# First batch of a windowed attention: probabilities held in the array, v with a column of ones moving, normalisation behind the product

## The chip, the cores and the metric

The kernel runs on one core of one Trainium2 chip. The metric is device time in microseconds (us) of one execution; three executions of the kernel before took 1189.88 to 1190.43 us, median 1190.07. The engines are named as in the profile: PE is TensorE's matrix array, PEld its loading of the operand that stays in the array, DVE is VectorE, ACT is ScalarE, POOL is GpSimd, SP is the queue that issues most transfers.

## The reference, cut to what matters

Attention over 4 batches, 8 heads, 768 positions, head size 64, where each query sees its last `n_local` = 96 keys and the first `n_global` = 8 keys, with a bias that falls with distance; its output feeds a mixture of 4 experts with weights given per row.

```python
scores = scale * q @ k.T + bias[head]            # -1e9 where a key is not kept
a = np.exp(scores - max(scores))
a = a / (sum(a) + 1e-9)
x = concat_heads(a @ v)                          # 3072 x 512
out = sum_e p[:, e] * (relu(x @ w1[e]) @ w2[e])
```

## The kernel before, in words

Queries are worked in tiles of 128. A tile of queries needs one window of 256 keys at most: 96 earlier keys and 32 global ones, which stand as one block of 128, and its own 128. The first tile of a head needs its own 128 alone. Two heads (a pair) are worked together, so a batch is 4 pairs of 6 tiles.

The first batch is done by itself ahead of everything else (`attention(0, A, early=True)`, called at line 916). Its result x is needed before the mixture can begin. The attention of the batches 1 to 3 runs beside the mixture's products of the batch before it, in another form that the change leaves alone. While the first batch runs, the steps (one tile each, 24 of them in the pair order 0, 2, 1, 3, and 4 more to empty the pipeline) also carry chores, at fixed step numbers (lines 917 to 928): the first expert weights are loaded and split into two parts on ACT and POOL, and the blocks of x that the mixture's products need are formed on DVE, ACT and POOL. `Ordered` keeps each engine's instructions in the order in which the program writes them, so an instruction that waits holds all that stand behind it on that engine.

The stages of one tile in the first batch, one step apart:

- `scores_early` (line 401), every second step: for two tiles and two heads, q times k on PE. k and q of 64 rows each, one head in each half of the array's rows.
- `softmax` (line 414) with the tile as `new`: one DVE instruction per head adds the bias and takes the maximum, then ACT takes the exponential and its sum (`accum_out`, which the trace shows as a second, short ACT instruction).
- `softmax` one step later with the tile as `old`: DVE adds 1e-9 to the sums, takes the reciprocal and multiplies the 256 probabilities of each head by it.
- `turn` (line 455) one step later: PE transposes the four 128x128 blocks of probabilities, ACT copies them from PSUM to pT.
- `weigh` (line 467), once in three tiles: v (128 keys x 64) stands in the array and pT (128 keys x 128 queries) moves, so the output is already x with head dimension down the partitions; the two heads use the two halves of the array's columns. One ACT copy takes 384 columns of x out of PSUM.

`prepare_early` (line 361) transposes q and k in threes on PE and copies them out of PSUM on ACT. `windows` (line 378) forms the keys' block of 96 earlier and 32 global rows of v by one transfer and one POOL copy. `load` (line 308) issues v's transfer on SP. The table `AHEAD` (line 212) says in which steps a later pair is prepared. PSUM holds one buffer for px, three for the transposes and four for the scores (line 915). fp32 products of PE appear as two instructions per product in the trace, transposes as one.

Of the kernel before, what the change touches and what calls it, by code (L numbers as in the profile page):

```python
# [9 lines left out]
F32 = mybir.dt.float32  # L10
# [3 lines left out]
AF = mybir.ActivationFunctionType  # L14
ALU = mybir.AluOpType
# [3 lines left out]
P = 128  # L19
NEG = 1.0e9  # L20

NGLOB = 32
NPREV = 96
# [163 lines left out]
def attn_moe_kernel(ctx: ExitStack, tc, q, k, v, n_global, n_local, domain_probs, w1, w2, out):  # L187
    nc = tc.nc
    B, H, S, D = q.shape
    N, E = domain_probs.shape  # L190
    DM, FF = w1.shape[1], w1.shape[2]
    NQT = S // P
# [4 lines left out]
    HALF = S // 2  # L197
# [110 lines left out]
    def load(A, src, b, pr, name, parts=1):  # L308

        if src is v:  # L310
            nat = A.natv.tile([P, 2, NQT, D], F32, name=name)
            rows = src[b, 2 * pr : 2 * pr + 2].rearrange("j (t p) d -> p (j t) d", p=P)
            sy.dma_start(nat.rearrange("p j t d -> p (j t) d"), rows)
            yield nat
            return
        nat = A.nat.tile([P, NQT, 2, D], F32, name=name)
        for hf in range(parts):
            ts = slice(hf * NQT // parts, (hf + 1) * NQT // parts)
            for j in range(2):
# [38 lines left out]
        if hf == 0:  # L358
            ve.tensor_copy(kd[:, :, :, P:], f32(kd[:, :, 0:1, :NGLOB]).to_broadcast([P, 2, NQT, NGLOB]))

    def prepare_early(A, nat, hf, name, got):

        tp = transpose_half(A, nat, hf)
        tpv = tp[:, :HALF].rearrange("p (t c) -> p t c", c=P)
        pl = slice(hf * TPH, (hf + 1) * TPH)
        if name == "q":
            if hf == 0:
                got["q"] = A.qd.tile([P, NQT, P], F32, name="early_q")
            ac.activation(got["q"][:, pl, :], tpv, AF.Copy, scale=-SCALE)
            return  # L370
        if hf == 0:
            got["k"] = A.kd.tile([P, NQT, PL], F32, name="early_k")
        dst = got["k"]
        ac.copy(dst[:, pl, :P], tpv)
        if hf == 0:
            po.tensor_copy(dst[:, :, P:], dst[:, 0:1, :NGLOB].to_broadcast([P, NQT, NGLOB]))

    def windows(A, vt):

        vg = A.vg.tile([P, 2, NQT, D], F32, name="vg")  # L380
        sy.dma_start(vg[:NPREV], vt[NGLOB:])
        po.tensor_copy(vg[NPREV:], vt[:NGLOB, :, 0:1, :].to_broadcast([NGLOB, 2, NQT, D]))
        return vg

    def scores(A, t, got):
# [15 lines left out]
    def scores_early(A, t0, got):  # L401
# [9 lines left out]
                te.matmul(heads[j][:, t - t0, :n], got["q"][own, t, :], win, start=True, stop=True)  # L411
        return [[heads[j][:, i] for j in range(2)] for i in range(2)]

    def softmax(A, new, old):


        if old:
            pb, zsum = old["pb"], old["zsum"]
        if new:
            t, pr, ps = new["t"], new["pr"], new["ps"]  # L420
            cols = slice(0, P) if t == 0 else slice(0, 2 * P)
            bcol = slice(2 * P, 3 * P) if t == 0 else slice(0, 2 * P)
            new["pcol"] = pcol = slice(P, 2 * P) if t == 0 else slice(0, 2 * P)
            nmax = A.small.tile([P, 2], F32, name="nmax")
            new["zsum"] = A.small.tile([P, 2], F32, name="zsum")
            new["pb"] = A.pb.tile([P, 2, 2 * P], F32, name="pb")
        for j in range(2):
            if new:
                e = new["pb"][:, j, pcol]
                ve.tensor_tensor_reduce(  # L430
                    e, ps[j][:, cols], nbias[:, 2 * pr + j, bcol], 1.0, 3.0e38, ALU.add, ALU.min, nmax[:, j : j + 1]
                )
                ac.activation(
                    e, e, AF.Exp, bias=nmax[:, j : j + 1], scale=-1.0, accum_out=new["zsum"][:, j : j + 1]
                )
            if old:
                if j == 1:
                    ve.reciprocal(zsum, zsum)
                elif A.early:

                    old["spare"] = spare = A.small.tile([P, 3], F32, name="spare")
                    ve.tensor_scalar(zsum, zsum, 1e-9, None, op0=ALU.add, op1=ALU.add, accum_out=spare[:, 2:3])
                else:
                    ac.activation(zsum, zsum, AF.Copy, bias=1e-9)
        if old:
            for j in range(2):
                p = pb[:, j, old["pcol"]]
                if A.early:
                    ve.tensor_scalar(
                        p, p, zsum[:, j : j + 1], None, op0=ALU.mult, op1=ALU.add, accum_out=old["spare"][:, j : j + 1]  # L450
                    )
                else:
                    ac.activation(p, p, AF.Copy, scale=zsum[:, j : j + 1])
# [12 lines left out]

    def weigh(A, three, x):

# [18 lines left out]
    def attention(b, A, early=False):  # L487


        x = xs[b] = xp.tile([P, NPAIR, S], F32, name="x")  # L490
        tiles, turned, ahead = [None] * 4, [], [None]

        def flow(new=None):

            one, two, three, four = tiles
            if new:
                if not early:
                    new["ps"] = scores(A, new["t"], gots[new["pr"]])
                elif new["t"] % 2 == 0:
                    new["ps"], ahead[0] = scores_early(A, new["t"], gots[new["pr"]])  # L500
                else:
                    new["ps"] = ahead[0]
            if four:
                turned.append(four)
            ready = len(turned) == TPH
            if ready and not early:
                weigh(A, turned, x)
            if three and not early:
                turn(A, three)
            softmax(A, one, two)  # L510
            if three and early:
                turn(A, three)
            if ready and early:
                weigh(A, turned, x)
            if ready:
                turned.clear()
            tiles[:] = [new, one, two, three]

        def start(pr):
# [17 lines left out]

        def prepare_all(pr):

            nat, got = nats[pr], gots[pr]  # L540
            got["v"] = nat
            prepare_early(A, nat["q"], 0, "q", got)
            if pr:
                yield 1
            prepare_early(A, nat["k"], 0, "k", got)
            yield 1
            nat["vg"] = windows(A, nat["v"])
            prepare_early(A, nat["k"], 1, "k", got)
            yield 1
            prepare_early(A, nat["q"], 1, "q", got)  # L550
            yield 1

        nats, gots = {}, [{} for _ in range(NPAIR)]
# [463 lines left out]
```

## Time and profile before

| | |
|---|---|
| median of three runs | 1190.07 us (1189.88 to 1190.43) |
| span of the profiled execution | 1189.2 us |
| instructions | 18,091 |
| PE busy | 1164.3 us, 98% of the span |
| PEld busy | 1039.9 us, 87% |
| DVE busy | 825.8 us, 69% |
| ACT busy | 494.4 us, 42% |
| POOL busy | 210.7 us, 18% |
| HBM | 190 GB/s over the span |

The page gives no time for the profiled execution but its span from first to last instruction; the median of the runs is 0.87 us above that span. The span has two parts. To about 63 us the first batch's attention runs by itself with the chores; after it the mixture's products fill PE to the end. A busy PE in the profile need not be PE at its peak, since each instruction's time holds the array's latency and neighbours overlap; how closely instructions follow one another is read from their start times in the timeline.

### The profile page before, as it was taken

How to read it: one execution, taken by the hardware profiler on the slowest of the kernel's cores; microseconds unless marked ns; L12 is line 12 of the kernel's file. 1: busy time of each engine (PE TensorE's matmuls, PEld its weight loads, DVE VectorE, ACT ScalarE, POOL GpSimd, SP SyncE). 2: the span in 40 equal slices, each digit the busy share in tenths (PEclk: the TensorE clock that was granted, in tenths of full speed). 3: DMA queues.
4: the chain of work that ended last, by engine and by line, in shares of the span. 5: the costliest groups of instructions: out<-in, count | busy, mean ns of one | idle time of the engine just before them, and what ended most of it. 6: DMA issues, size and time to landing. Idle time of an engine off the chain costs nothing.

```text
span 1189.2 us, 18091 instructions
## 1 busy us (share of the span) xinstructions
PE 1164.3 (98%) x6624; PEld 1039.9 (87%) x6624; DVE 825.8 (69%) x1859; ACT 494.4 (42%) x1268; POOL 210.7 (18%) x221
## 2 busy tenths in 40 slices
PE   7789999999999999999999999999999999999998
PEld 5579899898989898998988998989988999999996
DVE  7887676776687666666758867666666766666665
ACT  7955655565533444444432444444444211111110
POOL 4755665555230000000001000000001000000000
PEclk9999999999999999999999999999999999999999
DMA  8486897878578566666657657575654645554532
GB/s 200 160 246 243 306 299 264 258 278 298 178 244 275 186 209 198 201 217 213 183 178 242 237 198 219 164 238 192 206 186 154 234 188 195 195 187 177 186 133 91
DMA packets 122703, 251.38 MB, mean 211 GB/s; under 512 B 83184, under 2 KB 91376, under 8 KB 106224
## 3 DMA queue, kind: packets, MB, share of 16 engines
q1 hardware_dynamic: 118864, 243.87, 61.8%
q10 hardware_dynamic: 3744, 6.30, 1.4%
q8 instruction: 54, 0.88, 0.3%
q14 instruction: 41, 0.34, 0.1%
HBM read 174.11 MB, written 52.43 MB: 190 GB/s over the span
## 4 chain that ended last, share of the span: by engine, by line
PE 90%; DMA 3%; ACT 3%; DVE 2%; POOL 1%; issue 1%; SPq 0%; POOLq 0%; DVEq 0%
PE pm L43 80%; PE pt L43 6%; PE ps L43 3%; DMA qd<-st_q 2%; ACT pb L43 1%; DVE pb L43 1%; DMA raw<-in_moe_w_dram 1%; POOL w1s L43 0%; DMA q<-in_q_dram 0%; ACT xT L43 0%; ACT pT L43 0%; SPq L43 0%; DVE x L43 0%; ACT w1s L43 0%; POOL w2s L43 0%
## 5 line engine op out<-in xcount | busy, mean ns | idle before, releaser
L43 PE MATMUL pm<-w2s,h 128*128 128x512 f32 x2304 | 551.6, 393 | 1.5 <-DVE h L43 1.5
L43 PEld LDWEIGHTS pm<-w2s,h 128*128 128x128 f32 x2304 | 426.1, 188 | 89.4 <-DVE h L43 3.1
L43 DVE SCALAR_TENSOR_TENSOR acc<-pm,prob,acc 128x512 f32<-128x512 f32 x360 | 267.8, 749 | 151.6 <-PE pm L43 149.7
L43 PE MATMUL pm<-xT,w1s 128*128 128x384 f32 x1536 | 296.0, 337 | 1.7 <-DVE vv L43 1.0
L43 PEld LDWEIGHTS pm<-xT,w1s 128*128 128x128 f32 x1536 | 266.3, 188 | 5.2 <-issue 1.7
L43 PE MATMUL pm<-xB,w1s 128*128 128x384 f32 x1146 | 225.2, 338 | 0.2 <-DVE xB L43 0.2
L43 PEld LDWEIGHTS pm<-xB,w1s 128*128 128x128 f32 x1146 | 200.4, 188 | 5.1 <-issue 0.5
L43 ACT ACTIVATE h<-pm 128x384 fp32r<-128x384 f32 x256 | 124.7, 491 | 176.5 <-DVE pm L43 172.8
L43 DVE SCALAR_TENSOR_TENSOR h<-pm,h 128x384 fp32r<-128x384 f32 x256 | 140.5, 551 | 10.9 <-ACT h L43 7.7
L43 ACT ACTIVATE pb<-pb,nmax 128x256 f32<-128x256 f32 (+1 forms) x192 | 93.8, 495 | 92.1 <-DVE nmax L43 91.2
L43 ACT COPY p<-pm 128x384 f32<-128x384 f32 x63 | 30.2, 479 | 185.8 <-PE pm L43 176.9
L43 POOL COPY vg<-v 32x768 f32<-32x768 f32 x16 | 13.5, 843 | 505.5 <-DMA v<-in_v_dram 440.4
L43 DVE TENSOR_TENSOR u<-pm,p 128x384 f32<-128x384 f32 x64 | 35.6, 557 | 71.2 <-PE pm L43 58.1
L43 DVE CUSTOM_DVE_ANT_0 pb<-ps,nbias 128x256 f32<-128x256 f32 (+1 forms) x192 | 71.5, 396 | 8.3 <-PE ps L43 4.8
L43 ACT COPY pT<-pt 128x512 f32<-128x512 f32 (+1 forms) x96 | 53.4, 556 | 53.6 <-PE pt L43 53.4
L43 DVE TENSOR_TENSOR pm<-pm,vv 128x384 f32<-128x384 f32 x128 | 71.6, 560 | 1.5 <-PE pm L43 1.3
L43 ACT ACTIVATE pb<-pb,zsum 128x256 f32<-128x256 f32 (+1 forms) x144 | 63.3, 484 | 17.9 <-DVE zsum L43 17.8
L43 PE MATMUL pt<-ident,pb 128*128 128x128 f32 x352 | 57.4, 278 | 7.7 <-DVE pb L43 5.4
L43 PEld LDWEIGHTS pt<-ident,pb 128*128 128x128 f32 x352 | 42.1, 141 | 17.8 <-ACT pb L43 3.3
L43 DVE TENSOR_TENSOR vv<-pm,u 128x384 f32<-128x384 f32 x64 | 35.6, 557 | 27.3 <-PE pm L43 26.9
L43 DVE TENSOR_TENSOR u<-pm,u 128x384 f32<-128x384 f32 x64 | 35.6, 557 | 27.1 <-PE pm L43 26.5
L43 POOL TENSOR_TENSOR w2s<-raw,w2s 128x512 fp32r<-128x512 f32 x32 | 40.9, 1293 | 44.8 <-ACT w2s L43 44.7
(91 smaller groups left out, 881.3 us busy)
## 6 DMA issues: line engine op xcount, KB each, us to landing
w1s<-kept SPq DMA_DIRECT2D x48, 1792.0 KB, 7.3
w2s<-kept SPq DMA_DIRECT2D x48, 1024.0 KB, 4.8
kept<-w1s SPq DMA_DIRECT2D x16, 1792.0 KB, 7.9
qd<-st_q SPq DMA_DIRECT2D x96, 192.0 KB, 5.0
raw<-in_moe_w_dram SPq DMA_DIRECT2D x32, 512.0 KB, 4.7
kept<-w2s SPq DMA_DIRECT2D x16, 1024.0 KB, 6.6
v<-in_v_dram SPq DMA_DIRECT2D x16, 384.0 KB, 4.0
out_dram<-acc ACTq DMA_DIRECT2D x24, 256.0 KB, 3.4
```

Source lines behind the costliest of these rows:

```text
L43: ins = fn(*args, **kwargs)
```

## The change

In the first batch alone, the probabilities are no longer normalised before they are transposed. The transposed probabilities (128 keys x 128 queries) now stand in the array and v moves, 64 columns and one more that holds ones; so the output has queries down the partitions, 64 columns of unnormalised x and one of the sum, for each of the two heads. Once in three tiles DVE adds 1e-9 to the sums, takes the reciprocal and multiplies the three tiles' x by it; PE then transposes x back in three transposes in the step after, and DVE (for the last pair ACT) copies it to x. The exponential no longer sums. q and k of all pairs but the first are copied out of PSUM by DVE where ACT did it. v's tile has 65 columns per head and tile, and POOL writes the ones. The other batches' code is the same as before (in `softmax` only the branch for the first batch is taken out).

```diff
     def load(A, src, b, pr, name, parts=1):
         if src is v:
-            nat = A.natv.tile([P, 2, NQT, D], F32, name=name)
+            nat = A.natv.tile([P, 2, NQT, D + 1 if A.early else D], F32, name=name)
             rows = src[b, 2 * pr : 2 * pr + 2].rearrange("j (t p) d -> p (j t) d", p=P)
-            sy.dma_start(nat.rearrange("p j t d -> p (j t) d"), rows)
+            if A.early:
+                po.memset(nat[:, :, :, D:], 1.0)
+            sy.dma_start(nat[:, :, :, :D].rearrange("p j t d -> p (j t) d"), rows)
...
-    def prepare_early(A, nat, hf, name, got):
+    def prepare_early(A, nat, hf, name, got, lead):
...
-            ac.activation(got["q"][:, pl, :], tpv, AF.Copy, scale=-SCALE)
+            if lead:
+                ac.activation(got["q"][:, pl, :], tpv, AF.Copy, scale=-SCALE)
+            else:
+                ve.tensor_scalar_mul(got["q"][:, pl, :], tpv, -SCALE)
...
-        ac.copy(dst[:, pl, :P], tpv)
+        if lead:
+            ac.copy(dst[:, pl, :P], tpv)
+        else:
+            ve.tensor_copy(dst[:, pl, :P], tpv)
...
+    def exponentials(A, new, j):
...
+        ve.tensor_tensor_reduce(e, ps[j][:, cols], nbias[:, 2 * pr + j, bcol], 1.0, 3.0e38, ALU.add, ALU.min, nmax)
+        if A.early:
+            ac.activation(e, e, AF.Exp, bias=nmax, scale=-1.0)
+        else:
+            ac.activation(e, e, AF.Exp, bias=nmax, scale=-1.0, accum_out=new["zsum"][:, j : j + 1])
...
-                    ve.tensor_scalar(zsum, zsum, 1e-9, None, op0=ALU.add, op1=ALU.add, accum_out=spare[:, 2:3])
...
-                    ve.tensor_scalar(
-                        p, p, zsum[:, j : j + 1], None, op0=ALU.mult, op1=ALU.add, accum_out=old["spare"][:, j : j + 1]
-                    )
...
+    def weigh_early(A, tile_, px):
+
+        t, pT = tile_["t"], tile_["pT"]
+        vt, vg = tile_["v"]["v"], tile_["v"]["vg"]
+        for j in range(2):
+            for w in range(1 if t == 0 else 0, 2):
+                vv = vt[:, j, t] if w == 1 else vg[:, j, t - 1]
+                te.matmul(
+                    px[:, t % TPH, j], pT[:, w, j, :], vv, start=(w == 1 if t == 0 else w == 0), stop=(w == 1)
+                )
+
+    def normalise(A, px):
+
+        z = A.small.tile([P, TPH, 2, 1], F32, name="z")
+        xn = A.pb.tile([P, TPH, 2, D], F32, name="xn")
+        ve.tensor_scalar_add(z, px[:, :, :, D:], 1e-9)
+        ve.reciprocal(z, z)
+        ve.tensor_tensor(xn, px[:, :, :, :D], z.to_broadcast([P, TPH, 2, D]), op=ALU.mult)
+        return xn
+
+    def turn_values(A, xn, x, pr, hf):
+
+        tp = A.pt.tile([P, 512], F32, name="pt")
+        for i in range(TPH):
+            te.transpose(tp[:, i * P : (i + 1) * P], xn[:, i].rearrange("p j d -> p (j d)"), ident)
+        dst = x[:, pr, hf * HALF : (hf + 1) * HALF]
+        if pr == PAIRS[-1]:
+            ac.copy(dst, tp[:, :HALF])
+        else:
+            ve.tensor_copy(dst, tp[:, :HALF])
...
+        def flow_early(new=None):
+
+            one, two, three, four = tiles
+            if normed:
+                turn_values(A, *normed.pop())
+            if new:
+                if new["t"] % 2 == 0:
+                    new["ps"], ahead[0] = scores_early(A, new["t"], gots[new["pr"]])
+                else:
+                    new["ps"] = ahead[0]
+            if one:
+                for j in range(2):
+                    exponentials(A, one, j)
+            if two:
+                turn(A, two)
+            if three:
+                if three["t"] % TPH == 0:
+                    ahead.append(A.px.tile([P, TPH, 2, D + 1], F32, name=A.pxname))
+                weigh_early(A, three, ahead[1])
+                if three["t"] % TPH == TPH - 1:
+                    normed.append((normalise(A, ahead.pop()), x, three["pr"], three["t"] // TPH))
+            tiles[:] = [new, one, two, three]
```

`windows` takes v's new width (65) for its tile, its transfer and its POOL copy, and `prepare_all` passes `lead`, true for the first pair.

## Rows read from the trace of the kernel before

**Rows 1.** The profile's page: the span and the busy time of each engine.
```profile
span 1189.2 us, 18091 instructions
PE 1164.3 (98%) x6624; PEld 1039.9 (87%) x6624; DVE 825.8 (69%) x1859; ACT 494.4 (42%) x1268; POOL 210.7 (18%) x221
```

**Rows 2.** The chain of work that ended last, its last piece (start, length, what).
```profile
918.78 264.67 PE pm L43 x1320
```

**Rows 3.** Busy time of each engine in stretches of 10 us; after the stretch and its length stand PE, PEld, DVE, ACT and POOL, each with its instructions, then the granted clock, DMA's share and GB/s.
```profile
20.00:30.00 10.00, 9.87 (x95) 7.58 (x95) 9.31 (x61) 10.00 (x36) 4.04 (x5) 1.00 0.75 191
...
40.00:50.00 10.00, 6.73 (x48) 4.48 (x46) 8.30 (x39) 8.23 (x27) 8.78 (x10) 0.83 0.84 322
```

**Rows 4.** PE's timeline in the first batch, from the first transposes of probabilities to the end of the stage (start us, length us, engine, line, operation, out<-in, shapes, count); a next group's start less this group's start is what the group took of PE.
```profile
12.59 0.50 PE L43 MATMUL pt<-ident,pb 128*128 128x128 f32 x2 [0.27 <-DVE pb L43]
...
21.02 1.13 PE L43 MATMUL ps<-early_k,early_q 64*128 64x256 f32 x8
...
23.22 0.44 PE L43 MATMUL px<-pT,vg 128*64 128x128 f32 x4
...
24.68 0.55 PE L43 MATMUL pt<-ident,k 128*128 128x128 f32 x3
25.16 1.13 PE L43 MATMUL ps<-early_k,early_q 64*128 64x256 f32 x8
26.23 0.66 PE L43 MATMUL pt<-ident,pb 128*128 128x128 f32 x4
26.72 0.49 PE L43 MATMUL pt<-ident,q 128*128 128x128 f32 x3
27.05 0.60 PE L43 MATMUL pt<-ident,pb 128*128 128x128 f32 x4
...
31.89 1.14 PE L43 MATMUL ps<-early_k,early_q 64*128 64x256 f32 x8
...
59.91 1.30 PE L43 MATMUL ps<-xB,w1s 128*128 128x384 f32 x6
61.06 0.85 PE L43 MATMUL pt<-ident,pb 128*128 128x128 f32 x4
...
63.34 0.97 PE L43 MATMUL pm<-xB,w1s 128*128 128x384 f32 x4
```

**Rows 5.** ACT's timeline in one step of the first batch (columns as in the group before).
```profile
25.81 0.53 ACT L43 COPY early_k<-pt 128x384 f32<-128x384 f32 x1
26.18 0.57 ACT L43 ACTIVATE pb<-pb,nmax 128x256 f32<-128x256 f32 x1
26.59 0.25 ACT L43 ACTIVATION_READ_ACCUMULATOR pb<-pb,nmax 128x1 f32 x1
26.68 0.56 ACT L43 ACTIVATE pb<-pb,nmax 128x256 f32<-128x256 f32 x1
...
27.18 0.63 ACT L43 COPY pT<-pt 128x512 f32<-128x512 f32 x1
27.64 0.56 ACT L43 ACTIVATE early_q<-pt 128x384 f32<-128x384 f32 x1
```

**Rows 6.** DVE's groups of instructions between 9 and 64 us, different shapes apart (busy us, mean ns of one, idle before).
```profile
L43 DVE TENSOR_SCALAR_CACHE_REDUCE pb<-pb,zsum 128x256 f32<-128x256 f32 x40 | 17.6, 477 | 0.7
...
L43 DVE RECIPROCAL zsum<-zsum 128x2 f32<-128x2 f32 x24 | 3.8, 159 | 0.0
L43 DVE TENSOR_SCALAR_CACHE_REDUCE zsum<-zsum 128x2 f32<-128x2 f32 x24 | 3.6, 151 | 4.6 <-ACT pb L43 4.4
```

**Rows 7.** The costliest groups of instructions on the page (busy us, mean ns of one, idle before): loads and products of the mixture, and a DVE instruction that reads 384 columns of PSUM.
```profile
L43 PE MATMUL pm<-w2s,h 128*128 128x512 f32 x2304 | 551.6, 393 | 1.5 <-DVE h L43 1.5
L43 PEld LDWEIGHTS pm<-w2s,h 128*128 128x128 f32 x2304 | 426.1, 188 | 89.4 <-DVE h L43 3.1
...
L43 DVE TENSOR_TENSOR u<-pm,p 128x384 f32<-128x384 f32 x64 | 35.6, 557 | 71.2 <-PE pm L43 58.1
```

**Rows 8.** Instructions that write the tiles px and ps in the first 64 us: count, shortest/median/longest duration in ns, first and last start, shapes.
```profile
L43 PEld LDWEIGHTS px<-pT,v x96: 132/137/232, 18.5 to 63.0; 128*64 128x64 f32 x96
L43 PE MATMUL px<-pT,v x96: 272/273/473, 18.5 to 63.1; 128*64 128x128 f32 x96
...
L43 PEld LDWEIGHTS ps<-early_k,early_q x96: 182/187/335, 7.4 to 53.3; 64*128 64x128 f32 x96
L43 PE MATMUL ps<-early_k,early_q x96: 272/376/792, 7.4 to 53.5; 64*128 64x256 f32 x80, 64*128 64x128 f32 x16
```

**Rows 9.** PE's timeline in the mixture: four products of scores of the later batches, 256 columns moving, between products of 512 columns.
```profile
89.63 0.64 PE L43 MATMUL ps<-kd,qd 128*128 128x256 f32 x4
90.10 1.09 PE L43 MATMUL pm<-w2s,h 128*128 128x512 f32 x4
```

**Rows 10.** ACT's timeline at and behind the end of the stage.
```profile
63.46 0.48 ACT L43 COPY x<-px 128x384 f32<-128x384 f32 x1 [0.34 <-PE px L43]
...
71.16 0.62 ACT L43 CAST w2s<-raw 128x512 fp32r<-128x512 f32 x1 [0.82 <-DMA raw<-in_moe_w_dram]
```

**Rows 11.** The timeline of loads (PEld) where a group of px begins behind transposes.
```profile
29.41 0.20 PEld L43 LDWEIGHTS px<-pT,v 128*64 128x64 f32 x4 [0.17 <-issue]
```

**Rows 12.** POOL's timeline: the first of its chores on the expert weights and the last in this stage.
```profile
31.92 0.73 POOL L43 TENSOR_TENSOR sums<-raw 128x256 f32<-128x256 f32 x1 [6.30 <-DMA raw<-in_moe_w_dram]
...
61.44 1.27 POOL L43 TENSOR_TENSOR w1s<-sums,w1s 128x512 fp32r<-128x512 f32 x1
```

More of the change, by code (lines that the diff above doesn't have):

```diff
@@ L412, in scores_early @@
         return [[heads[j][:, i] for j in range(2)] for i in range(2)]
-    def softmax(A, new, old):
[L417 to L426, printed above, removed]
+    def exponentials(A, new, j):
+        t, pr, ps = new["t"], new["pr"], new["ps"]
+        cols = slice(0, P) if t == 0 else slice(0, 2 * P)
+        bcol = slice(2 * P, 3 * P) if t == 0 else slice(0, 2 * P)
+        if j == 0:
+            new["pcol"] = slice(P, 2 * P) if t == 0 else slice(0, 2 * P)
+            new["nmax"] = A.small.tile([P, 2], F32, name="nmax")
+            new["pb"] = A.pb.tile([P, 2, 2 * P], F32, name="pb")
+            if not A.early:
+                new["zsum"] = A.small.tile([P, 2], F32, name="zsum")
+        e, nmax = new["pb"][:, j, new["pcol"]], new["nmax"][:, j : j + 1]
+        ve.tensor_tensor_reduce(e, ps[j][:, cols], nbias[:, 2 * pr + j, bcol], 1.0, 3.0e38, ALU.add, ALU.min, nmax)
[3 more added lines that the diff above has]
+            ac.activation(e, e, AF.Exp, bias=nmax, scale=-1.0, accum_out=new["zsum"][:, j : j + 1])
@@ L427, in softmax @@
+    def softmax(A, new, old):
         for j in range(2):
             if new:
[L429 to L435 removed]
+                exponentials(A, new, j)
@@ L490, in attention @@
         x = xs[b] = xp.tile([P, NPAIR, S], F32, name="x")
-        tiles, turned, ahead = [None] * 4, [], [None]
-        def flow(new=None):
+        tiles, turned, ahead, normed = [None] * 4, [], [None], []
+        def flow_early(new=None):
             one, two, three, four = tiles
+            if normed:
+                turn_values(A, *normed.pop())
             if new:
-                if not early:
-                    new["ps"] = scores(A, new["t"], gots[new["pr"]])
-                elif new["t"] % 2 == 0:
+                if new["t"] % 2 == 0:
                     new["ps"], ahead[0] = scores_early(A, new["t"], gots[new["pr"]])
@@ L502, in flow @@
                     new["ps"] = ahead[0]
+            if one:
[10 more added lines that the diff above has]
+            tiles[:] = [new, one, two, three]
+        def flow(new=None):
+            if early:
+                return flow_early(new)
+            one, two, three, four = tiles
+            if new:
+                new["ps"] = scores(A, new["t"], gots[new["pr"]])
             if four:
                 turned.append(four)
-            ready = len(turned) == TPH
-            if ready and not early:
+            if len(turned) == TPH:
                 weigh(A, turned, x)
-            if three and not early:
+                turned.clear()
+            if three:
                 turn(A, three)
             softmax(A, one, two)
[L511 to L516, printed above, removed]
             tiles[:] = [new, one, two, three]
```

28 lines of the change are left out of this document (12 added, 16 removed).

## The prediction, made before the changed kernel was run

> **What bounds the kernel now.** I read the page first: PE is busy 98% of the span [rows 1], so the change can matter only where PE has gaps or gets other work. The chain of waits ends in 264.67 us of nothing but products [rows 2]; the mixture behind the first batch is PE from end to end, and the change leaves its products alone. So the time moves by what the first batch's stage, which ends at about 63 us, gets shorter or longer.
>
> In that stage the table of stretches names two engines. From 20 to 30 us ACT is busy 10.00 of 10 and PE 9.87; from 40 to 50 PE is down to 6.73 and the granted clock to 0.83 [rows 3]. As "busy" counts overlapped latency, I went on to the starts in PE's timeline [rows 4]. Eight instructions of scores take 25.16 to 26.23 = 1.07 us, four transposes 26.23 to 26.72 = 0.49, three of q or k 26.72 to 27.05 = 0.33, and 24 of px 23.22 to 24.68 = 1.46, or 0.061 each. The six tiles from 21.02 to 31.89 need 3 x 1.07 + 22 x 0.122 + 44 x 0.061 + 6 x 0.33 = 10.6 us of such work, in 10.87 us. So in the first half PE is as full as ACT. Over the stage, from the first transposes of probabilities at 12.59 to the last px, behind which the next product starts at 63.34, PE has 50.75 us and needs: scores 10 x 1.07 = 10.7, transposes 88 x 0.122 = 10.8, px 176 x 0.061 = 10.7, twelve groups of q and k 4.0, the opening product 59.91 to 61.06 = 1.15; together 37.4 us. The other 13.4 us are waits and a slow clock, nearly all in the second half, where ACT and POOL carry the chores.
>
> **What the change takes away.** On ACT the short instruction behind each exponential goes: from exponential to exponential it is 0.50 us with it, 26.18 to 26.68, and 0.41 up to its start at 26.59 [rows 5]; 0.09 x 48 = 4.3 us. Twelve copies of q and k (25.81 to 26.18 = 0.37) and six of x go to DVE: 18 x 0.37 = 6.7 us. An attention tile then costs ACT 2 x 0.41 + 0.46 = 1.3 us. On DVE two multiplications of 477 ns, the 1e-9 (151) and the reciprocal (159) go per tile [rows 6], some 1.26 us. In come, per three tiles, 1e-9, reciprocal and one multiplication (557 by an instruction that reads 384 columns of PSUM [rows 7]), and the 18 copies, 0.56 each by the same row: (0.87 x 8 + 0.56 x 18) / 24 = 0.71 per tile. Both engines are relieved. Where PE is the bound that is worth nothing; in all it is worth at most PE's 13.4 us.
>
> **What it adds on PE: the pace of px.** The count of 176 instructions stays. Before, 64 columns of v are loaded and 128 columns move, and the two heads share the array. After, 128 columns are loaded and 65 move, and each product takes the whole array. Moving: 128 columns take 273 ns and 256 take 376 [rows 8], 0.8 ns a column, so 65 columns stream in about 53 ns, which is per product what two at a time cost today. Loading: 64 columns take 137 ns and 128 take 187 [rows 8], again 0.8 ns a column, so 128 columns stream in about 100 ns. No row shows a load longer than the product that covers it. Bounds: 0.061, today's pace, if the load doesn't count, and 0.153, if load and product follow one another. The nearest row has a 128-column load behind a stream of about equal length: four products in 89.63 to 90.10, 0.118 each [rows 9]. That loads hide behind products is seen where 188 ns of load vanish under products of 512 columns [rows 7]. I take 0.118: 176 x (0.118 - 0.061) = +10.0 us.
>
> The Trainium skill speaks against this change: "TensorEngine Tiling (Array Packing)", section Performance Considerations, says that where the moving side has 64 columns or fewer the operands are to be swapped and the array's columns split, which is how the kernel stands before. "TensorE: Matmul & The Clock Gate", section LDWEIGHTS (loading the stationary operand), gives columns / 1.2 ns; an estimate by that page is 107 ns for 128 columns, and the term would be 176 x (0.107 - 0.061) = +8.1 in place of +10.0. The 50 ns between the loads of 64 and 128 columns agree with it.
>
> **The transposes back.** Eight groups of three, 0.33 each [rows 4]: +2.6 us.
>
> **A new wait.** PE keeps program order, and the transposes back stand at the head of the step behind normalisation. They wait for the last px's latency (273 ns less 53 for 63 columns fewer: 0.22), for DVE's 0.15 + 0.16 + 0.56 [rows 6, 7] and for two hand-overs of 0.05, as from px to the copy of x at 63.46 [rows 10], an estimate: 1.19, less 0.1 for px's own slot, 1.1 us. Behind them on PE stand that step's scores, transposes and px, and ACT and DVE wait for those. Eight times is 8.8; in three of the eight the table AHEAD puts three transposes of q or k (0.33) in between: +7.8 us. Bounds: 0, if other work of PE fills it all, and 9 to 10, if DVE is late with its copies. In the kernel before normalisation lies a step ahead of the transposes and costs PE little while it is full.
>
> **What comes back.** With no split columns the 0.17 us of idle loading ahead of a px group [rows 11] should go: 8 x 0.17 = -1.4 us; bounds 0 and twice that, were the way back as dear.
>
> **Small edits.** POOL's writes of ones hold v's loads on SP. The fourth pair's must wait until the first pair's v is free; behind it stand k's global columns on POOL and the expert weights' first loads on SP, which arrive some 2 us later for it. POOL's chores, 31.92 to 62.71 [rows 12], would begin later and are covered by PE's later end. If PE were not late, that cover were gone: POOL is busy 8.78 us of 10 from 40 on [rows 3], so its chain can shrink little, and a stage that ended before about 60 would meet it. The wider copy and transfer of v's window (780 columns for 768) I take as nothing; POOL hides it.
>
> **Sum.** 37.4 + 10.0 + 2.6 + 7.8 - 1.4 = 56.4 us, from 12.6: the last transposes end at 69.0 and the copy of x starts 0.2 later, at 69.2, where it starts at 63.46 now [rows 10]: +5.75. This leaves PE no other wait, as both other engines need under 2 us a tile for 2.35 on PE. Behind the stage, ACT waits 0.82 us for a weight load [rows 10] whose issue hangs on an earlier step and not on the end; I take 0.5 back. The span gets 5.25 longer, 1194.45; the median lies 0.87 above the span now, so the time is **1195.3 us**. All terms are at full clock; the slow stretch after 40 us [rows 3] came with PE's gaps, which go.
>
> **Rivals.**
> 1. *Faster: the load does not pace px.* If 128 columns of load hide as 64 do today, px stays at 0.061, and the end moves by 5.25 - 10.0 = -4.75: 1185.3, or up to 1188 where POOL's chores then hold it. For it: loads of 137 ns already follow at 0.061. Against it: the 0.118 [rows 9]. The sign turns at 0.118 - 5.25 / 176 = 0.088. Chance 0.20.
> 2. *Much slower: load and product take turns.* At 0.153, 176 x 0.035 = 6.2 more: 1201.5. The Trainium skill's "TensorE: Matmul & The Clock Gate", Part 3, lets a load overlap a running product in other rows of the array or in a background buffer; its first half alone would make it this rival. For it: every load is now to the whole array. Against it: the 188 ns hidden under products of the whole array [rows 7]. Chance 0.10.
> 3. *Nothing to be measured: the new work falls into the 13.4 us.* The second half's waits for ACT and POOL stay, and its half of the added work (10 us) lies beside them; the first half's lies beside the wait for normalisation where AHEAD fills it. End at +1 to +2: 1191.5. Against it: in my sum the relief of ACT takes those waits away first. Chance 0.10.
>
> The forecast has 0.60, from 1192 (pace 0.107, the new wait 0.9) to 1199 (pace 0.13, DVE late with its copies).
>
> **How the numbers follow.** The forecast's own 1192 to 1199 leaves out 4 in 10. To hold 8 the range takes in rival 3, half of rival 1 down to 1186.5, and rival 2 up to 1202. A measurement of this kernel tells 0.2%, 2.4 us, from no change. Slower: the forecast but 0.05 at its low end, and rival 2: 0.65. Within: that 0.05, rival 3 and nothing of rival 1 but its POOL-bound end, 0.03: 0.18. Faster: the rest of rival 1: 0.17.
>
> **What would show it.** Right: px instructions about 0.12 us apart with loads of 187 ns; eight idle times of PE of about a microsecond ahead of the transposes of xn, put down to DVE; ACT with idle time between 20 and 30 us; the scores that start at 31.89 [rows 4] some 7 us later; the last copy of x at about 69. Wrong: px 0.06 apart; PE waiting for ACT, POOL or DVE's chores in the second half as now; or a last copy of x at 63 or before.

## The result: slower by 12 us, more than twice what was forecast

The changed kernel takes 1202.28 us (median of 4 runs, 1200.85 to 1204.60) where the kernel before takes 1190.25 on the same chip: ratio 1.0097, 95% interval 1.0082 to 1.0112. The forecast was 1195.3, range 1186.5 to 1202.0: the sign holds, the size does not, and the time lies 0.3 us above the range. The profiled run took 1200.85 us with a span of 1198.1.

The page after, against [rows 1], and the last piece of its chain, against [rows 2]: the span has grown by 8.9 us, and the last run of products starts 8.93 later and is as long as before. So all of it lies ahead.

```profile
span 1198.1 us, 17947 instructions
```

```profile
927.71 264.65 PE pm L43 x1320
```

Stretches of the stage, columns as in [rows 3]. Between 20 and 30 us ACT has fallen from 10.00 to 4.01 and DVE from 9.31 to 6.47: the relief is there. But PE has fallen as well, from 9.87 to 8.86, and the low clock, in the kernel before at 42 to 48 us, is still there, at 51 to 57. The first line below is the kernel before, the others the changed one.

```profile
42.00:45.00 3.00, 3.00 (x22) 2.47 (x24) 2.96 (x13) 3.00 (x12) 1.99 (x2) 0.52 0.83 350
```

```profile
20.00:30.00 10.00, 8.86 (x76) 7.58 (x76) 6.47 (x25) 4.01 (x10) 4.79 (x6) 1.00 0.68 151
...
51.00:54.00 3.00, 2.98 (x16) 2.16 (x17) 2.19 (x7) 1.32 (x3) 2.51 (x3) 0.59 1.06 415
54.00:57.00 3.00, 3.00 (x25) 2.91 (x26) 2.23 (x10) 2.27 (x6) 2.74 (x4) 0.84 1.01 414
```

PE's timeline, against [rows 4]:

```profile
12.99 1.34 PE L43 MATMUL pt<-ident,pb 128*128 128x128 f32 x6
...
20.40 0.52 PE L43 MATMUL pt<-ident,xn 128*128 128x128 f32 x3 [0.83 <-DVE xn L43]
20.85 0.93 PE L43 MATMUL ps<-early_k,early_q 64*128 64x128 f32 x8
21.71 0.66 PE L43 MATMUL pt<-ident,pb 128*128 128x128 f32 x4
22.20 0.34 PE L43 MATMUL px<-vg,pT 128*128 128x65 f32 x2
22.37 0.39 PE L43 MATMUL px<-v,pT 128*128 128x65 f32 x2
...
23.04 0.50 PE L43 MATMUL pt<-ident,q 128*128 128x128 f32 x3
...
40.16 1.14 PE L43 MATMUL ps<-early_k,early_q 64*128 64x256 f32 x8
...
47.39 0.39 PE L43 MATMUL px<-v,pT 128*128 128x65 f32 x2
47.98 0.95 PE L43 MATMUL pt<-ident,pb 128*128 128x128 f32 x4 [0.20 <-ACT pb L43]
48.84 0.44 PE L43 MATMUL px<-vg,pT 128*128 128x65 f32 x2
...
49.56 0.39 PE L43 MATMUL px<-v,pT 128*128 128x65 f32 x2
51.02 0.55 PE L43 MATMUL pt<-ident,xn 128*128 128x128 f32 x3 [1.07 <-DVE xn L43]
51.50 1.65 PE L43 MATMUL ps<-early_k,early_q 64*128 64x128 f32 x8
53.08 1.11 PE L43 MATMUL pt<-ident,pb 128*128 128x128 f32 x4
53.99 0.53 PE L43 MATMUL px<-vg,pT 128*128 128x65 f32 x2
...
55.29 0.61 PE L43 MATMUL pt<-ident,pb 128*128 128x128 f32 x4
...
72.66 0.39 PE L43 MATMUL px<-v,pT 128*128 128x65 f32 x2
74.21 0.52 PE L43 MATMUL pt<-ident,xn 128*128 128x128 f32 x3 [1.16 <-DVE xn L43]
74.48 1.83 PE L43 MATMUL pm<-xB,w1s 128*128 128x384 f32 x9
```

Four things are to be seen. Eight instructions of px take 22.20 to 23.04 = 0.84 us, 0.105 each (0.111 behind the first pair: 22.37 to 23.04 for six). The last pair of px ahead of a normalisation starts at 72.66 and takes 0.22 of PE, as the pairs before it do, so its slot ends at 72.88; PE's next start is at 74.21, 1.33 us later. At 47.98 PE waits for ACT, which the forecast had excluded. And behind the wait that ends at 51.02 the same eight instructions of scores that took 0.86 at 20.85 take 1.58. The scores that started at 31.89 start at 40.16, 8.3 later, where the forecast had said 7.

The wait for ACT has its beginning on DVE. In the timelines of DVE and of ACT, DVE's copy of x (44.16) stands ahead of the next biases (44.64). ACT, idle for 1.91 us until the first maximum arrives, then has its chores `w1s` and `w2s` ahead of the next exponentials, which start at 47.41; PE needs them at 47.61.

```profile
44.16 0.56 DVE L43 COPY x<-pt 128x384 f32<-128x384 f32 x1 [0.17 <-PE pt L43]
44.64 0.41 DVE L43 CUSTOM_DVE_ANT_0 pb<-ps,nbias 128x256 f32<-128x256 f32 x1
```

```profile
45.09 0.91 ACT L43 ACTIVATE pb<-pb,nmax 128x256 f32<-128x256 f32 x2 [1.91 <-DVE nmax L43]
...
46.37 0.62 ACT L43 CAST w1s<-sums 128x512 fp32r<-128x512 f32 x1
46.89 0.62 ACT L43 CAST w2s<-raw 128x512 fp32r<-128x512 f32 x1
47.41 0.91 ACT L43 ACTIVATE pb<-pb,nmax 128x256 f32<-128x256 f32 x2
```

What PE waited for between 12 and 76 us (total, times, longest). The idle time counted here begins when the last product has left the array, so it is shorter than the time lost between starts.

```profile
PE pt L43 <- DVE xn L43: 8.1, 8, 1.2
PE pt L43 <- ACT pb L43: 0.4, 2, 0.2
```

The instructions on the tile px (against [rows 8]): the load takes 192 ns for 137 before, as it has 128 columns; the product 275 for 273, though it has half the columns.

```profile
L43 PEld LDWEIGHTS px<-v,pT x96: 186/192/333, 14.1 to 72.7; 128*128 128x128 f32 x96
L43 PE MATMUL px<-v,pT x96: 223/275/418, 14.2 to 72.8; 128*128 128x65 f32 x96
...
L43 DVE TENSOR_SCALAR z<-px x8: 164/165/166, 19.3 to 73.1; 128x6 f32<-128x6 f32 x8
L43 DVE TENSOR_TENSOR xn<-px,z x8: 556/558/558, 19.7 to 73.5; 128x384 f32<-128x384 f32 x8
```

The stage's end on ACT, against [rows 10]: the last copy of x starts at 74.77, which was 63.46.

```profile
74.77 0.48 ACT L43 COPY x<-pt 128x384 f32<-128x384 f32 x1 [1.63 <-PE pt L43]
```

That is 11.31 later, and the span is 8.9 longer: 2.4 come back behind the stage. Some 0.5 of it is back when the mixture's second products start (84.06 before, 94.91 after); of the rest 1.2 is a wait of PE for q's transfers of the later batches, which over the whole trace comes to 1.4 us before and 0.2 after.

### The profile page after: what moved, and what is told of

It reads as the page before. It is cut to its first block, busy times and chain, and to the rows that moved or that the text cites. A ratio compares the mean times of both kernels' runs of the same rounds, so it can differ in the third digit from the quotient of the medians.

```text
span 1198.1 us, 17947 instructions
## 1 busy us (share of the span) xinstructions
PE 1173.8 (98%) x6648; PEld 1053.2 (88%) x6648; DVE 816.4 (68%) x1733; ACT 484.1 (40%) x1202; POOL 211.3 (18%) x225
## 4 chain that ended last, share of the span: by engine, by line
PE 95%; DVE 2%; ACT 1%; DMA 1%; issue 1%; SPq 0%; DVEq 0%; ACTq 0%
PE pm L43 81%; PE pt L43 8%; PE ps L43 4%; PE px L43 1%; DMA qd<-st_q 1%; DVE xn L43 0%; DMA q<-in_q_dram 0%; DVE x L43 0%; ACT xT L43 0%; DVE z L43 0%; ACT pb L43 0%; DVE h L43 0%; DVE pb L43 0%; ACT xB L43 0%; DVE pm L43 0%
## 5 line engine op out<-in xcount | busy, mean ns | idle before, releaser
L43 ACT ACTIVATE pb<-pb,nmax 128x256 f32<-128x256 f32 (+1 forms) x192 | 90.8, 486 | 109.3 <-DVE nmax L43 108.3
L43 POOL COPY vg<-v 32x768 f32<-32x768 f32 (+1 forms) x16 | 13.7, 855 | 500.9 <-DMA v<-in_v_dram 440.0
L43 DVE TENSOR_TENSOR u<-pm,p 128x384 f32<-128x384 f32 x64 | 35.6, 557 | 69.2 <-PE pm L43 57.0
```

The costliest lines, as they stand in the source:

```text
L43: ins = fn(*args, **kwargs)
```

## The experiments

The theory after the first comparison (A in the expectations): PE's own work was sized right; the rest of the loss is that the transposes back stand at the head of PE's step and wait there, that DVE's copy of x ahead of the biases makes ACT late, and that PE's gaps let its clock fall. Against it stood that the load does not set px's pace, that the copies of q and k on DVE cost the time, and that the loss has nothing to do with the exchanged product; the other letters are rivals of this kind. All ratios are to the kernel before on the same chip.

**The changed kernel once more.** No edit.

> The changed kernel once more, beside the others of this group and the kernel before. Ratio to the kernel before about 1.010 (1.008 to 1.011) by every theory. It shows besides how far the time lies above the span in both kernels on one chip: 0.9 us in the profiled execution of the kernel before, 2.7 us in that of the changed one.

1202.47 us, ratio 1.0093 (1.0078 to 1.0108). The profiled run took 1205.15, and its copy of x started at 77.56. Its stretches show why:

```profile
66.00:81.00 15.00, 13.75 (x56) 13.62 (x57) 4.71 (x14) 5.59 (x13) 3.51 (x4) 0.50 0.79 246
```

The slow stretch has moved to 66 to 81 us and is longer. The eight runs of this kernel spread from 1200.85 to 1205.15, the longest at a mean clock of 0.991, the shortest at 0.997.

**The transposes back behind the next step's px**, with two buffers for px and two, not three, for the transposes.

```diff
-            if normed:
-                turn_values(A, *normed.pop())
+            due = normed.pop() if normed else None
...
                 weigh_early(A, three, ahead[1])
+            if due:
+                turn_values(A, *due)
+            if three:
                 if three["t"] % TPH == TPH - 1:
...
-        A = Pools(start_stack, "start", ..., ps=2, pt=3, px=1, early=True)
+        A = Pools(start_stack, "start", ..., ps=2, pt=2, px=2, early=True)
```

> The transposes back and the copy of x stand behind the next step's products, px has two buffers of PSUM and the transposes two in place of three. Theory A (the wait for normalisation at the head of PE's step is the largest single term, 9.4 us in eight waits in the changed kernel's trace, and the copy of x ahead of the next bias and maximum makes ACT late on top): the waits are gone, the stage ends 8 to 11 us earlier, the time falls to 1.001 to 1.004 of the kernel before. Theory B (PE's added work alone makes the time, the waits only show where work would be late anyway): less than 3 us comes back, 1.008 or more. The one buffer fewer for transposes may cost up to 1.5 us by either.

1198.69 us, ratio 1.0066 (1.0053 to 1.0080): less came back than theory A expected, and more than theory B. The waits for normalisation are gone but for one, yet others have come with the missing buffer:

```profile
PE pt L43 <- DVE x L43: 2.0, 3, 0.7
PE pt L43 <- ACT pT L43: 1.4, 3, 0.7
PE pt L43 <- DVE xn L43: 1.2, 1, 1.2
```

So this run says nothing on the price of the wait alone.

**Only DVE's copy of x behind the next biases**; the transposes back stay at the head.

```diff
             te.transpose(tp[:, i * P : (i + 1) * P], xn[:, i].rearrange("p j d -> p (j d)"), ident)
+        yield
         dst = x[:, pr, hf * HALF : (hf + 1) * HALF]
...
-            if normed:
-                turn_values(A, *normed.pop())
+            back = turn_values(A, *normed.pop()) if normed else iter(())
+            next(back, None)
...
             if one:
                 for j in range(2):
                     exponentials(A, one, j)
+            next(back, None)
```

> The transposes back stay at the head of PE's step; the copy of x out of PSUM on DVE stands behind the next tile's bias and maximum instead of ahead of it. Theory A (in the second half the chain from the transposes back over DVE's copy to the exponential makes PE wait for ACT): 1.5 to 3 us come back, ratio 1.007 to 1.009, and the idle times of PE put down to ACT's exponentials around 48 and 64 us go. Theory B: no change, within 0.7 us of the changed kernel.

1198.77 us, ratio 1.0067 (1.0053 to 1.0081): 3.7 us back, more than expected. In PE's waits the eight for normalisation stand as they were, those for the exponentials are down to 0.3, and in the stretches the clock of the stage is whole, with the eight waits still there:

```profile
PE pt L43 <- DVE xn L43: 8.1, 8, 1.2
PE px L43 <- ACT pb L43: 0.3, 1, 0.3
```

```profile
51.00:60.00 9.00, 7.83 (x69) 6.63 (x66) 6.76 (x26) 7.27 (x18) 7.78 (x9) 1.00 0.83 256
```

ACT's lateness belonged to the place of that copy: four transposes of probabilities that took 0.86 us behind ACT's exponentials take 0.49 in the same step here. In this one profiled run the stage's slow clock went with it; a slow stretch came behind the stage, at 90 to 96 us (0.72).

**The transposes back left out**: x is copied from the normalised tile as it stands.

```diff
-        tp = A.pt.tile([P, 512], F32, name="pt")
-        for i in range(TPH):
-            te.transpose(tp[:, i * P : (i + 1) * P], xn[:, i].rearrange("p j d -> p (j d)"), ident)
+        tp = xn.rearrange("p t j d -> p (t j d)")
```

> The transposes back are left out; x is filled from the normalised values as they stand (so x has the wrong layout). PE loses 24 transposes (2.9 us) and the wait at the head of the step, but the next step's first product still waits until normalisation has read px. Theory A: 7 to 10 us come back, ratio 1.001 to 1.004. Theory B: only the 2.9 us, 1.007 to 1.008.

1195.93 us, ratio 1.0043 (1.0030 to 1.0057): 6.5 less than the changed kernel, a little less than theory A asked. PE now waits for the one buffer of px (1.2 us) and for the exponentials (1.0): part of the removed wait only changes its name.

```profile
PE px L43 <- DVE xn L43: 1.2, 3, 0.5
...
PE pt L43 <- ACT pb L43: 1.0, 3, 0.4
```

**The old orientation, with all else as changed**: v stands in the array, products tile by tile, no normalisation, nothing transposed back.

```diff
-                te.matmul(px[:, t % TPH, j], pT[:, w, j, :], vv, ...)
+                te.matmul(px[j * D : (j + 1) * D, i * P : (i + 1) * P], vv, pT[:, w, j, :], ...)
```

> The products of px as in the kernel before (v stands, 64 columns loaded, 128 move, the heads share the array), all else of the change kept, but the normalisation and the transposes back are left out (x stays unnormalised) and DVE, for the last pair ACT, copies px to x. Theory A (PE's added work and waits make the time): PE is back at some 37 us of work in the stage and ACT and DVE are relieved; the stage ends at 58 to 62 us, where POOL's chores hold it: ratio 0.996 to 1.000. Theory L (the pace of px is not what costs; the kernel without transposes back, 1.0043, has shown the rest): 1.003 or more.

1191.73 us, ratio 1.0006 (0.9997 to 1.0015), a little above theory A's 1.000. Without the exchanged product there is no loss that the runs can tell; so the loss is the product's orientation and what hangs on it (normalisation behind it and the transposes back), and not the copies on DVE, POOL's ones or v's wider tile.

**Half the moving columns**: 33 of the 65 move, so 32 of each head's 64 columns of x are computed, and written twice.

```diff
-                vv = vt[:, j, t] if w == 1 else vg[:, j, t - 1]
+                vv = vt[:, j, t, 32:] if w == 1 else vg[:, j, t - 1, 32:]
```

> 33 columns move instead of 65 (v's last 32 and the ones; x gets the same 32 twice), the loads of 128 columns stay. Theory P (the load of 128 columns sets the pace of px): px stays at 0.105 to 0.112 us per instruction, ratio as the changed kernel, 1.008 to 1.0105. Rival Q (load and stream add): 32 columns less at 0.8 ns are 0.026 us, times 176 = 4.6 us less, ratio 1.0055.

The moving columns do not set the pace of px: eight take 22.63 to 23.44 = 0.81 us, 0.101 each, for 0.105 with twice the columns, and all of that difference is in the first pair; the six behind it take 22.77 to 23.44 = 0.67 us, as with 65. What stays the same is the load of 128 columns into the whole array; no run here tells these two apart.

```profile
22.63 0.31 PE L43 MATMUL px<-vg,pT 128*128 128x33 f32 x2
22.77 0.39 PE L43 MATMUL px<-v,pT 128*128 128x33 f32 x2
...
23.44 0.53 PE L43 MATMUL pt<-ident,q 128*128 128x128 f32 x3
```

The time is another matter: 1213.66 us, ratio 1.0199 (1.0185 to 1.0213), some 11 us more than with 65 columns, which no theory had. The stretches show the clock:

```profile
51.00:60.00 9.00, 8.66 (x43) 7.24 (x43) 4.73 (x17) 5.15 (x12) 7.31 (x9) 0.56 0.97 314
60.00:69.00 9.00, 7.83 (x36) 6.55 (x35) 4.09 (x17) 4.32 (x10) 2.43 (x3) 0.50 0.00 0
```

With the same order of work and the same eight waits (8.0 us for 8.1), and fewer columns in each product, PE spent most of 51 to 84 us at 1.2 GHz; all five runs have a mean clock of 0.980 to 0.987.

**All copies of q and k on ScalarE again.**

```diff
-            nat, got, lead = nats[pr], gots[pr], pr == PAIRS[0]
+            nat, got, lead = nats[pr], gots[pr], True
```

> All copies of q and k out of PSUM are ACT's again, as in the kernel before. Theory A (PE is the bound in the first half, where ten of the twelve moved groups lie): no change beyond 1.5 us, ratio 1.008 to 1.011. Rival R (DVE is late because of the copies that it took over, and normalisation with it): 2 us or more come back, 1.0075 or less.

1204.93 us, ratio 1.0101 (1.0084 to 1.0118): DVE's share of the copies is not the cause. Its two runs with a clock of 0.997 or more have spans of 1199.0 us, as the changed kernel's 1198.1 to 1199.1 in its five runs at such a clock. What did change is the time outside of the span: 1.73 to 1.86 us, for 2.8 to 3.2.

**Transposes back and copy behind the next step's scores, biases and turns**, ahead of its px; the buffers as in the change.

```diff
-            if normed:
-                turn_values(A, *normed.pop())
+            due = normed.pop() if normed else None
...
             if two:
                 turn(A, two)
+            if due:
+                turn_values(A, *due)
             if three:
```

> The transposes back and the copy of x stand behind the next step's scores, bias, maximum and transposes of probabilities, but ahead of its px; px keeps one buffer and the transposes three. The wait for normalisation is then filled by 0.49 us of transposes, and in every second case by 1.07 of scores. Theory A: of 9.4 us of waits 4 to 6 go and DVE's copy is no longer ahead of the bias: 1.002 to 1.004. Theory C (the copy's place alone makes ACT late and the clock low; what PE gains otherwise meets ACT and POOL in the second half): as with the copy alone moved, 1.0055 to 1.007.

1193.71 us, ratio 1.0023 (1.0014 to 1.0033): this is 2.3 us above the kernel before on its chip, where the changed kernel is 11.8 above it on its own; some 9 us are back by the place of three transposes and a copy. Four waits for normalisation are left, 2.2 us; no stretch of the stage is at the lower clock (mean 0.999), and the last copy of x starts at 67.38. PE still waits for late exponentials within its groups: four transposes take 0.87 from 44.37 and 0.84 from 48.79, for 0.44.

```profile
PE pt L43 <- DVE xn L43: 2.2, 4, 1.2
```

```profile
67.38 0.48 ACT L43 COPY x<-pt 128x384 f32<-128x384 f32 x1 [1.64 <-PE pt L43]
```

**The wait filled**: five products nobody reads, ahead of the transposes back.

```diff
         tp = A.pt.tile([P, 512], F32, name="pt")
+        for _ in range(5):
+            te.matmul(tp[:, HALF:], ident, ident, start=True, stop=True)
```

> The changed kernel, with five more 128-column products of the identity with itself (their result is read by nobody) ahead of each step's transposes back, where TensorE waits for the normalised values. Theory C (the idle waits let TensorE's clock fall in this stage, and that is 2 to 4 us of what the changed kernel lost): no stretch of granted clock 0.50 in the stage, mean clock 0.998 or more, 0.5 to 2 us of added work paid where the wait was shorter than the filling; 1196 to 1200 us, ratio 1.005 to 1.008, and its runs lie within 1.5 us. Theory S (the clock falls for another reason, the waits only stand beside it): 1202 to 1205, ratio 1.009 to 1.012, spread as before.

1200.09 us, ratio 1.0077 (1.0063 to 1.0090), with runs from 1198.95 to 1200.16 and clocks of 0.999 and 1.000. PE shows no wait for normalisation, and the stretches that were at 0.59 and 0.84 are whole:

```profile
51.00:54.00 3.00, 3.00 (x27) 2.40 (x27) 2.18 (x8) 1.88 (x5) 2.31 (x4) 1.00 1.14 444
54.00:57.00 3.00, 3.00 (x27) 2.56 (x27) 2.56 (x10) 2.06 (x6) 2.92 (x4) 1.00 0.94 388
```

Useless work in the gaps makes the kernel faster by about 2 us, and steadier. So in this kernel the clock holds when the gaps are filled. That the gaps alone make it fall is not shown: with the same eight waits the stage was at full clock in the profiled run where only the copy had moved, and far longer at the low one with 33 moving columns. What else decides stays open. The intervals of this run and of the changed kernel overlap a little; that all five runs lie below all eight of the other is the stronger sign.

**The better place, with the copies of q and k on ScalarE.** The edits of the two kernels above.

> The kernel with the transposes back and the copy of x behind the next step's scores, biases and turns (1193.7 us), and the copies of q and k for every pair on ScalarE again. Theory O (the copies on VectorE cost about 1 us outside of the span, 2.7 to 3.0 instead of 1.8): outside of the span 1.7 to 1.9, span as there (1190.5 to 1191.5), 1192 to 1193 us, ratio 1.001 to 1.002. Theory R (ScalarE, with the copies, is late with the exponentials again): waits of TensorE for ScalarE grow, span 1192 or more, ratio 1.0025 to 1.005.

1193.08 us, ratio 1.0023 (1.0013 to 1.0032). Outside of the span the eleven runs have 1.74 to 1.90 us, as theory O said, where the kernel with the copies on DVE has 2.51 to 2.94. But the ratio is as before, a little above that theory's range: against the kernel before on the same chip the median span is 2.5 us longer here (1191.3 for 1188.8) and 1.5 there (1191.0 for 1189.5). What left the outside came back inside, and the two cannot be told apart in time. No version here that computes the attention beats the kernel before.

**The old orientation with three tiles' products at once**, as the kernel before groups them; again no normalisation.

```diff
-                weigh_early(A, three, ahead[1])
+                turned.append(three)
+                if len(turned) == TPH:
+                    px = A.px.tile([P, 512], F32, name=A.pxname)
+                    for tile_ in turned:
+                        weigh_early(A, tile_, px)
```

> The first attention in its old orientation (v stands, the transposed probabilities move, nothing transposed back), products of three tiles at once as before the change, everything else as changed: q and k copies on VectorE, no normalisation at all (left out, so the values are not the attention's). Theory A (the relief of VectorE and ScalarE is worth what TensorE's own waits for them were, little, since TensorE's work sets the stage): 1187 to 1191 us, ratio 0.997 to 1.000, last transposes of the stage's values at 61.5 to 63.5 us. Rival (something else than these two holds the stage, so that the relief is worth nothing): 1190.5 to 1192, ratio 1.000 to 1.0015, stage ends at 63.5 as before.

Ratio 0.9993 (0.9984 to 1.0003); the median span is 1187.4 for 1188.8, and the last copy of x starts at 62.45, for 63.46. All the relief of ACT and DVE in the old orientation, normalisation left out altogether, is worth 1.4 us of span, and 0.9 of that is lost outside of it.

**The kernel before with the exchanged product alone**: probabilities normalised as before, 64 columns of v move, ACT copies the product, PE transposes it back a step later.

```diff
+                    te.matmul(px[:, i, j], pT[:, w, j, :], vv, start=(w == 1 if t == 0 else w == 0), stop=(w == 1))
+        xn = A.pb.tile([P, TPH, 2, D], F32, name="xn")
+        ac.copy(xn, px)
...
+            if normed:
+                turn_values(A, *normed.pop())
...
-                weigh(A, turned, x)
+                normed.append(weigh_swapped(A, turned, x))
```

> The kernel before with only the orientation of the first attention's product exchanged: probabilities normalised as before and standing transposed in the array, v moving with its 64 columns, the product copied by ScalarE, transposed back and copied by ScalarE in the step after. So TensorE's cost comes without the relief of VectorE and ScalarE. Theory A (TensorE's added work is some 12 us of the stage, and ScalarE, full in the stage's first half, gets a copy more per step): 1200 to 1210 us, ratio 1.008 to 1.017. Rival (the relief mattered little, and the place of the transposes back all): as the kernel that has them further back, ratio 1.002 to 1.006.

1201.10 us, ratio 1.0094 (1.0079 to 1.0110), the last copy of x at 74.98. The waits now are the old ones, for the normalised probabilities, and new ones for ACT's copy; and the clock is low again, 0.50 to 0.67 from 54 to 66 us, behind the longest of these waits:

```profile
PE pt L43 <- DVE pb L43: 4.1, 4, 1.7
PE pt L43 <- ACT xn L43: 2.1, 3, 0.8
```

```profile
57.00:60.00 3.00, 3.00 (x16) 3.00 (x15) 1.93 (x12) 0.38 (x3) 0.00 (x0) 0.50 0.00 0
```

The exchanged product costs as much alone as in the whole change: as the change places it, what it relieves and what waiting it adds cancel. Its transposes back stand where the kernel with ratio 1.0023 has them, behind the step's transposes of probabilities and ahead of px, and it is still 0.7% slower than that one. So the better place is cheap only together with the relief of ACT and DVE, which in the old orientation was worth little; as the two kernels also differ in how they group px, the size of this is not exact.

## Why the prediction was right in kind and too small

**Right: what decides.** What the exchanged product adds on PE is what costs, its moving columns do not pace px, and the relief of ACT and DVE by itself is worth next to nothing (1.4 us of span, the old orientation with grouped products). The rival that px stays at today's pace is refuted by 0.105 us per instruction for 0.061, and 0.101 with half the columns; the one in which load and product take turns asked for 0.153.

**Right: the work.** px takes 20 tiles of eight at 0.84 and four of four at about 0.43, together 18.5 us; the sum had 10.7 + 10.0 - 1.4 = 19.3. The pace was lower than the 0.118 taken from a group with the same load and 256 moving columns. The sum also counted all ten groups of scores at 1.07; the three that begin a pair of heads have fewer columns and take 0.86 (20.85 to 21.71), 0.6 us less in all, before as after. By the Trainium skill ("TensorE: Matmul & The Clock Gate", section LDWEIGHTS) an estimate for a load of 128 columns was 107 ns; the pace of px in the trace, 105 to 111, agrees, while a load's own duration there is 192. The Trainium skill's rule on operands to be swapped ("TensorEngine Tiling (Array Packing)", Performance Considerations) speaks for the orientation before; the two kernels that keep it bear this out, with ratios of 1.0006 and 0.9993 (without normalisation), where all that exchange it have 1.0023 or more.

**Wrong: "This leaves PE no other wait" and "All terms are at full clock".** From the first transposes at 12.99 to the first product behind the last ones at 74.48 PE has 61.5 us; the sum had 56.4. The copy of x at 74.77 was forecast for 69.2. Of the 5.6 us between, 5.5 are these:

| | forecast | measured | miss |
|---|---|---|---|
| first transposes of probabilities | 12.6 | 12.99 | +0.4 |
| PE's work | 48.6 | 48.4 (what the other rows leave) | -0.2 |
| eight waits for normalisation | 7.8 | 9.4 | +1.6 |
| waits for ACT's exponentials | 0 | 2.1 | +2.1 |
| lower clock, 51.0 to 55.3 us | 0 | 1.6 | +1.6 |

*The wait* was the mis-sized term. From the end of px's last slot to the transposes back it is 1.24 to 1.33 us in five steps, and 0.91 to 1.00 in the three that have transposes of q or k between, for 1.1 and 0.77. DVE's three instructions take 0.165 + 0.192 + 0.557 = 0.91 where 0.87 was taken, and the hand-overs about 0.25 where 0.10 was.

*The exponentials* were excluded by a mean, which was the step that failed here: each engine needs under 2 us a tile for 2.35 on PE. In the steps behind a normalisation DVE has the copy of x, a copy of q or k and the biases of the tile all at once, and the order written for it puts the copy first. 47.61 to 47.98 is PE's idle time for it, and the four transposes behind take 0.86 for 0.44, since the second head's exponential is not there either; with three more such places up to 70.00 it comes to 2.1. Putting the copy behind the biases removed them.

*The clock*: the forecast read the low clock of the kernel before as coming with PE's gaps, which the kernel with filled gaps bears out in part, and held that the gaps go, which is wrong: eight of about a microsecond come in. The scores at 51.50 take 1.58 for 0.86, the transposes 0.91 for 0.49, px 1.30 for 0.84, the transposes back 0.48 for 0.45 (20.40 to 20.85): 1.6 us in the profiled run. Other runs lost more.

*Outside of the span* the time grew by another 1.0 to 1.3 us. The forecast took 0.87 us between span and median as given, but the span was that of one execution and the median that of others; in every run of the kernel before the time lies 1.7 to 1.9 above its own span, and in nearly all with the copies of q and k on DVE 2.5 to 3.2. Two pairs of kernels that differ in those copies alone show it, but in one of them the span takes back what the outside gives. What happens in that microsecond no view shows; it stays open.

**Too small: what comes back** behind the stage, 2.4 us for 0.5. This is a miss in the other direction, and by luck it hid 1.9 of the 5.6 us. With it the miss of 7.0 us adds up: 5.6 in the stage, less 1.9 behind it, 1.0 by which the median span of the four runs (1199.1) exceeds that of the profiled one, and 2.3 outside of the span (3.2 for 0.87).

**The bill.** Of 12 us, some 9 is the place of the transposes back and of the copy of x, with the lost clock that hangs on it (8.3 to 8.8 by the ratios, from 1.0093 and 1.0097 to 1.0023; 9.5 by the medians on each chip). 1.0 lies outside of the span. What is left, some 1.5 us of span, is the price of the exchanged product where it is placed well and ACT and DVE are relieved: 11 us more work on PE, of which by this sum 7 fall into the 13.4 us in which PE had waited before, as the copy of x starts only 3.9 later. That was the third rival's mechanism; it needed another place for the transposes back. How the 9 divides between wait, lateness and clock can't be had from single edits: the copy alone gives 3.7, the filling alone about 2, and they overlap.

## What to carry to other kernels

Price a small tail (normalise, transpose back) by where it stands in the bottleneck engine's order: a three-instruction chain on another engine, waited for at the head of the step, cost about as much here as the doubled loading that the change was judged by (some 9 us for 8), and moving it by half a step gave back three quarters of the loss. Judge "no other wait" step by step and not by means per tile: what comes in once in three tiles meets what comes in once in two. And price a product with few moving columns by the columns that it loads: here halving the moving ones gave back next to nothing of its pace, so the work saved elsewhere had to be paid for there.

## What the runs showed of the hardware

- In the profiled runs of the changed kernel no wait of PE in the stage was longer than 1.3 us, one in three tiles, and the granted clock still went from 2.4 to 1.2 GHz for stretches of 4 to 15 us; with useless products in these gaps it stayed (0.999 and 1.000 over the span). The gaps are not the whole of it: with 33 moving columns for 65 the waits were the same and the clock much lower (0.980 to 0.987), so that less work took 11 us longer, and with the copy of x moved the waits were the same and the stage's clock whole.
- Halving the moving columns of a product with 128 loaded columns took its pace from 0.105 to 0.101 us only, and not at all behind the first pair of a group (0.111).
- The time that lies outside of the span is not constant: 1.8 us or about 2.8, by which engine twelve copies stand on; the cause is open.
